# A lag on the inputs of ScalarE's casts in a list schedule: attention followed by a gated two-layer network, on one core

## The chip, the cores and the metric

The kernel runs on one core of one Trainium2 chip. The core has five engines that work side by side, each through its own queue in the order in which the program wrote it: TensorE (PE in the profile, with PEld for its weight loads), VectorE (DVE), ScalarE (ACT), GpSimd (POOL) and SyncE (SP), which here only issues the transfers (DMA) between DRAM and on-chip memory. The metric is the time of one execution on the device in microseconds (us); less is better.

## The reference

```python
# q, k, v: (8 batches, 8 heads, 576 rows, 64); tau = 0.02
scores = q @ k.T / sqrt(64)
scores = where(scores >= max(scores) - tau, scores, -1e9)      # only the top band survives
attn   = exp(scores - max(scores)); attn = attn / (sum(attn) + 1e-9)
x      = (attn @ v)  ->  (4608 tokens, 512)                     # heads side by side
gate   = sigmoid(x @ w_gate); val = x @ w_val                   # w_gate, w_val: 512 x 1536
out    = (gate * val) @ w_out                                   # w_out: 1536 x 512
```

The kernel writes `out` transposed, 512 x 4608. Everything is float32; a product that must keep float32's precision is made of three products of halves: a value is split into a rounded high part and the rest, and high x high, high x low and low x high are added up.

## The kernel before

**The work.** Attention goes through 32 visits: 8 batches `b` times 4 pairs of heads `hp`. A visit has 9 tiles of 128 queries. For each tile TensorE makes the scores (`s`, line 661), VectorE their negative maximum (`st`, 668), ScalarE the exponentials (`p`, 682), VectorE the mask and the row sums (685), TensorE transposes `p` in four pieces (`tp`, 767) and ScalarE copies the transposed block out of PSUM (`pt`, 718); every second tile TensorE multiplies with `v` (`av`, 803), and ScalarE copies that to `xf` (718 again). Scores, transposes and `av` share a few PSUM banks: the next one can only start once ScalarE or VectorE has emptied a bank. In the text a visit is named by its two numbers, so (5, 0) is batch 5, pair 0.

Beside attention, TensorE works through the gated network (`m`, line 863, and `o`, line 906) for batches 0, 1 and 2, in units of 12 matmuls of 512 columns with one weight tile each (`wi`, `wo`, 512 KB, streamed from DRAM through nine slots `w`). When attention ends, the other batches follow in three rounds of two batches at a time (lines 1105 and 1170), by Strassen's scheme in Winograd's form, with seven products in place of eight.

**The sums.** That scheme needs sums and differences of weight blocks. They are made on the way: while batches 1 and 2 go through `m`, and batches 0 and 1 through `o`, two weight tiles that have been streamed anyway are also read by POOL, which makes two new tiles of them (`s0_...`, `s1_...`, also in `w` slots) in six additions (line 957). Then ScalarE rounds each new tile to its high part (the cast of line 968), POOL subtracts that from the tile (969), and SP stores the result in DRAM (lines 977 and 989). There are 18 such sums, so 36 casts. The operations of a sum have the key 1000, lower in priority than attention's and higher than the network's.

**x read back.** For batch 2 the attention result goes to DRAM (`xa`, line 1271), comes back into a `t2` buffer (1301), and is split into high and low part by `split_x`: a cast on ScalarE (813) and a subtraction on POOL (815). There are 4 such casts. For batches 0 and 1 the same function reads `xf` without a detour (8 casts).

**What sets the order.** The program is not written in the order in which it runs. Each operation is recorded by `op(engine, cost, key, ...)` with the buffers that it reads and writes. `Plan.run` then plays a list schedule: it keeps a clock, counts an engine as busy for the recorded cost, and on each engine starts the ready operation with the lowest key whose buffers have room. An operation becomes ready when the last of its inputs is done, plus a lag: `LAG` for the engine (0.3 for ScalarE) plus the operation's own `lag`, which no operation of the kernel before sets. The order of starts is the order in which the program is then written. On the chip each engine goes through its queue in that order, whatever the real times are: an instruction that has to wait holds everything behind it on its engine.

```python
for s in x.succ:
    lag = 0.0 if s.eng == x.eng else LAG[s.eng]
    s.ready = max(s.ready, now + lag + s.lag)
```

Of the kernel before, what the change touches and what calls it, by code (L numbers as in the profile page):

```python
# [20 lines left out]
def f32(ap):  # L21
    return ap.bitcast(F32)
# [21 lines left out]
class Plan:  # L44
# [10 lines left out]
    def buf(self, tag, shape, dtype, name, cls=None):  # L55
        return Buf(self, tag, shape, dtype, name, cls)
# [9 lines left out]
    def op(self, eng, cost, key, emit, reads=(), writes=(), also=(), leave=0, behind=None, after=(), lag=0.0):  # L66


        o = Op()
        o.eng, o.cost, o.emit, o.key, o.leave, o.lag = eng, cost, emit, key, leave, lag  # L70
        o.succ, o.seq, o.ready = [], len(self.ops), 0.0
        deps, bufs = set(after), []
        for group, write in ((reads, False), (writes, True)):
            for x in group:
                b, part = x if isinstance(x, tuple) else (x, None)
                for q, p, w in b.accesses:
                    if (write or w) and (p is None or part is None or p == part):
                        deps.add(q)
                if b not in bufs:
                    bufs.append(b)  # L80
        for group, write in ((reads, False), (writes, True)):
            for x in group:
                b, part = x if isinstance(x, tuple) else (x, None)
                b.accesses.append((o, part, write))
        for b in bufs:
            b.users += 1
        deps.discard(o)
        o.n_deps, o.next = len(deps), None
        if behind is not None:
            o.n_deps += 1  # L90
            behind.next = o
        for q in deps:
            q.succ.append(o)
        o.bufs, o.also = bufs, [b for b in also]
        self.ops.append(o)
        return o
# [191 lines left out]
TWOS = ((3, 4), (5, 6), (7, 8))  # L288

SUMS_IN, SUMS_OUT, SUM_KEY = {1: (0,), 2: (1,)}, {0: (0,), 1: (1,)}, 1000  # L290

AWAY = 2
AHEAD_TWO = 8
# [5 lines left out]
def act(n):  # L299
    return 0.19 + 0.0008 * n  # L300
# [6 lines left out]
def pool(n):  # L307
    return 0.2 + 0.0022 * n
# [7 lines left out]
def kernel(  # L316
# [25 lines left out]
    nc = tc.nc  # L342
# [10 lines left out]
    SM = NJ * P  # L353
# [81 lines left out]
    op, buf = plan.op, plan.buf  # L435
# [373 lines left out]
               reads=[pt, pl] + ([c.pt, c.pl] if last else []) + [vis.vs], writes=[av], also=[vis.xf])  # L809
            last_att[0] = copy(AV(vis.first), W, key, lambda: vis.xf.ap[:, c0 : c0 + W], av, (vis.xf, self.name))  # L810

    def split_x(x, c0, c1, xf, key):
        op("ACT", act(c1 - c0), key, lambda: nc.scalar.copy(x.ap[:, 0, c0:c1], xf.ap[:, : c1 - c0]),
           reads=[xf], writes=[(x, (0, c0))])
        op("POOL", pool(c1 - c0), key, lambda: nc.gpsimd.tensor_tensor(
            out=x.ap[:, 1, c0:c1], in0=xf.ap[:, : c1 - c0], in1=f32(x.ap[:, 0, c0:c1]), op=ALU.subtract
        ), reads=[xf, (x, (0, c0))], writes=[(x, (1, c0))])
# [110 lines left out]
    def streamed(blk, tag=""):  # L928
        return lambda f, i: stream(
            wi_d[f, i], lambda: wi_d[f, i].t.rearrange("p z c f -> p (z c f)"), f"wi{blk}_{f}_{i}{tag}"  # L930
        )
# [19 lines left out]
    def sums(name, x_u, x_v, full, half, put):  # L951

        u, v = (buf("w", [P, 2 * DM], F32R, f"s{j}_{name}") for j in range(2))
        key = SUM_KEY

        def add(cost, out, x, y, sign, reads, writes):
            op("POOL", cost, key, lambda: nc.gpsimd.tensor_tensor(  # L957
                out=f32(out()), in0=f32(x()), in1=f32(y()), op=ALU.add if sign > 0 else ALU.subtract
            ), reads=reads, writes=writes)

        for t, x in ((u, x_u), (v, x_v)):
            add(1.3, lambda t=t: full(t, 0), lambda x=x: full(x, 0), lambda x=x: full(x, 1), 1, [x], [t])
        add(1.0, lambda: half(u, 1, 0), lambda: half(v, 0, 0), lambda: half(v, 0, 1), 1, [v], [u])
        add(1.0, lambda: half(u, 1, 1), lambda: half(u, 1, 0), lambda: half(u, 0, 0), -1, [], [u])
        add(1.0, lambda: half(v, 1, 0), lambda: half(u, 0, 0), lambda: half(v, 0, 0), -1, [u], [v])
        add(1.0, lambda: half(v, 1, 1), lambda: half(u, 0, 1), lambda: half(u, 1, 1), -1, [u], [v])
        for k, t in enumerate((u, v)):
            op("ACT", act(512), key, lambda t=t: nc.scalar.copy(full(t, 0), f32(full(t, 1))), writes=[t])
            op("POOL", 1.3, key, lambda t=t: nc.gpsimd.tensor_tensor(
                out=full(t, 1), in0=f32(full(t, 1)), in1=f32(full(t, 0)), op=ALU.subtract  # L970
            ), writes=[t])
            put(k, t, key)

    def in_sums(f, i, u, v):
        def put(k, t, key):
            d = si_d[f, i, k]
            op("SP", 1.7, key, lambda: nc.sync.dma_start(
                out=d.t.rearrange("p z c f -> p (z c f)"), in_=f32(t.ap)
            ), reads=[t], writes=[d])

        view = lambda t: t.ap.rearrange("p (z c f) -> p z c f", z=2, c=ND)
        sums(f"{f}_{i}", u, v, lambda t, z: view(t)[:, z], lambda t, z, h: view(t)[:, z, 2 * h : 2 * h + 2], put)

    def out_sums(g, e, u, v):
        view = lambda t: t.ap.rearrange("p (f z c) -> p f z c", f=ND, z=2)

        def put(k, t, key):
            d = so_d[g, k]
            op("SP", 1.7, key, lambda: nc.sync.dma_start(
                out=d.t[:, :, e].rearrange("p s f z c -> p s (f z c)"),  # L990
                in_=f32(t.ap).rearrange("p (s f z c) -> p s (f z c)", s=2, f=2, z=2),
            ), reads=[t], writes=[(d, e)])

        sums(f"o{g}_{e}", u, v, lambda t, z: view(t)[:, :, z], lambda t, z, h: view(t)[:, 2 * h : 2 * h + 2, z], put)
# [233 lines left out]
    t = 0  # L1228
# [8 lines left out]
    xs, gs = {}, {}  # L1237
# [7 lines left out]
    def attention(vis):  # L1245
        vis.prepare(LEAD)
        t, c, groups = vis.first, None, []
        for h, tiles in vis.groups:
            g = Group(vis, h, tiles)
            groups.append((g, t))  # L1250
            for i in range(g.n):
                tile_steps(vis, g, i, t + i)
            t += g.n
            g.normalise(t - 1)
            for i in range(g.n):
                g.transpose(i, t - 1 + 0.1 * i)
            if h is None:
                c = g
            g.leftover_keys(t - 1 + 0.2)
            if h == 1:  # L1260
                g.output(c, t - 1 + 0.3)
        if vis.late:
            late_normalise(vis, t)
        b, hp = vis.b, vis.hp
        if b in two_of:
            i, j = two_of[b]
            op("SP", 0.9, t, lambda i=i, j=j: nc.sync.dma_start(
                out=xp_d[i][hp].t[:, :, j], in_=vis.xf.ap[:, :SM].rearrange("p (z s) -> p z s", z=2)
            ), reads=[vis.xf], writes=[(xp_d[i][hp], j)])
        elif b >= AWAY:  # L1270
            op("SP", 0.9, t, lambda: nc.sync.dma_start(out=xa_d[b, hp].t, in_=vis.xf.ap[:, :SM]),
               reads=[vis.xf], writes=[xa_d[b, hp]])
        else:
            xs[b, hp] = buf("x", [P, 2, SM], F32R, f"x{b}_{hp}")
            split_x(xs[b, hp], 0, SM, vis.xf, t)
        i, j = two_of[B]
        SQ = SL // 2
        op("SP", 0.3, t, lambda: nc.sync.dma_start(
            out=xp_d[i][hp].t[:, :, j, b * SQ : (b + 1) * SQ],
            in_=vis.xf.ap[:, SM:].rearrange("p (z s) -> p z s", z=2),  # L1280
        ), reads=[vis.xf], writes=[(xp_d[i][hp], (j, b))])

    def block(b):
        return [xs[b, hp] for hp in range(NPAIR)]

    def new_g(b):
        gs[b] = [buf("g", [P, 2, SM], F32R, f"g{b}_{f}") for f in range(NF)]
        return gs[b]
# [4 lines left out]
    for vis in todo:  # L1293
        attention(vis)
        b = vis.b
        if vis.hp == NPAIR - 1 and b not in two_of:
            if b >= AWAY:
                for hp in range(NPAIR):
                    xf = buf("t2", [P, SM], F32, f"xa{b}_{hp}")
                    xs[b, hp] = buf("x", [P, 2, SM], F32R, f"x{b}_{hp}")  # L1300
                    op("SP", 1.0, 0.5, lambda xf=xf, b=b, hp=hp: nc.sync.dma_start(out=xf.ap, in_=xa_d[b, hp].t),
                       reads=[xa_d[b, hp]], writes=[xf], also=[xs[b, hp]])
                    split_x(xs[b, hp], 0, SM, xf, 0.5)
            in_units(b, block(b), new_g(b), 0, SM, 0, own if b == 0 else streamed(b))
            out_units(b, gs[b])
    for i in range(len(TWOS)):
# [80 lines left out]
```

## Time and profile before

| What | Value |
|---|---|
| time, median of 3 runs | 1363.42 us (1363.32 to 1367.26) |
| profiled execution | span 1362.5 us from its first to its last instruction; the profile gives no other time of it |
| busy: PE, PEld, DVE, ACT, POOL | 1323.1, 1089.2, 942.9, 726.4, 452.9 us |
| mean granted TensorE clock | 0.992 |
| DMA | 322.37 MB, mean 237 GB/s |
| attention and network together | up to about 828 us |
| rounds of two batches | from 844 us on |

A row of a timeline has the start and the length in us, the engine, the source line, the operation, what it writes and reads, the shape and the count; brackets give how long the engine stood idle just before, and what ended that. A row of a window table has the stretch, its length, then for each engine the busy time and the number of instructions, and at the end the granted TensorE clock (1.00 is full speed), the share of time in which the 16 DMA engines were busy, and their rate in GB/s. A row of waits has who waited for whom, the total in us, how many times, and the longest. Names in the profile have their numbers left out (`s` for a sum's tile and also for scores: the line tells them apart).

### The profile page before, as it was taken

The page shows a single profiled execution, that of the slowest core. Times are in us where ns is not written, and L with a number is a line of the kernel's source. Part 1 is how long each engine was busy: PE and PEld are TensorE (multiplying, and loading weights), DVE is VectorE, ACT ScalarE, POOL GpSimd, SP SyncE. Part 2 cuts the span into 40 slices and gives each one's busy share as a digit, 9 for nine tenths or more (in the row PEclk, how much of TensorE's full clock was granted, in tenths as well). Part 3 has the DMA queues.
Part 4 walks back from the last instruction along what each step waited for, and adds up shares of the span by engine and source line. Part 5 has one row for each costly group of instructions (what it writes and reads, how often), then busy time and mean ns, then how long its engine had stood idle before and what let it go on. Part 6 is the DMA issues. An engine that isn't in the chain of part 4 may idle for free.

```text
span 1362.5 us, 23334 instructions
## 1 busy us (share of the span) xinstructions
PE 1323.1 (97%) x8290; PEld 1089.2 (80%) x8290; DVE 942.9 (69%) x1848; ACT 726.4 (53%) x1339; POOL 452.9 (33%) x419
## 2 busy tenths in 40 slices
PE   8879999999999998999999999999999999999998
PEld 5557888888877887888878887888888888888887
DVE  7888878677766775677667772746965569655594
ACT  7887777666666765666666552222532225322242
POOL 3575756714444532634544421111000110001100
PEclk9998999999999999999989999999999999999999
DMA  7799999899788787898788777765685656756563
GB/s 267 242 282 312 332 255 284 278 257 263 227 244 248 230 243 224 239 274 260 219 250 261 221 210 244 246 205 188 216 292 195 196 189 219 238 193 190 189 217 123
DMA packets 151612, 322.37 MB, mean 237 GB/s; under 512 B 30152, under 2 KB 57800, under 8 KB 151496
## 3 DMA queue, kind: packets, MB, share of 16 engines
q1 hardware_dynamic: 151352, 320.88, 76.6%
q8 instruction: 66, 1.08, 0.3%
q14 instruction: 50, 0.41, 0.1%
q10 hardware_dynamic: 144, 0.00, 0.0%
HBM read 212.93 MB, written 54.67 MB: 196 GB/s over the span
## 4 chain that ended last, share of the span: by engine, by line
PE 80%; DMA 9%; SPq 4%; ACT 2%; DVE 2%; issue 2%; POOL 2%; POOLq 0%; ACTq 0%; DVEq 0%
PE m L863 11%; PE qb L1105 11%; PE av L803 8%; PE qa L1105 7%; PE qc L1105 7%; PE s L661 7%; PE o L906 6%; PE tp L767 6%; PE rb L1170 5%; PE rc L1170 4%; PE ra L1170 4%; DMA rd<-turned 1%; PE s_l L661 1%; DMA xp<-xf 1%; DMA kd<-k 1%
## 5 line engine op out<-in xcount | busy, mean ns | idle before, releaser
L668 DVE TENSOR_REDUCE st<-s 128x1 f32<-128x576 f32 x256 | 192.2, 752 | 98.7 <-PE s L661 92.1
L685 DVE SCALAR_TENSOR_TENSOR p<-s,st,p 128x576 f32<-128x576 f32 x256 | 207.2, 812 | 45.5 <-ACT p L682 40.5
L682 ACT ACTIVATE p<-s,st 128x576 f32<-128x576 f32 x256 | 191.1, 749 | 32.8 <-DVE st L668 32.2
L718 ACT COPY pt<-tp 128x512 f32<-128x512 f32 x256 | 149.1, 586 | 96.3 <-PE tp L767 95.0
L661 PE MATMUL s<-kd,qd 128*128 128x288 f32 x928 | 169.4, 306 | 5.1 <-DVE p L685 4.3
L863 PE MATMUL m<-x,wi 128*128 128x512 f32 x576 | 165.5, 409 | 1.4 <-ACT pt L718 1.4
L767 PE MATMUL tp<-ident,p 128*128 128x128 f32 x1024 | 157.4, 278 | 7.0 <-ACT xf L718 3.8
L1018 POOL TENSOR_TENSOR gA<-gA 128x512 f32<-128x512 f32 x18 | 24.1, 1341 | 406.8 <-DVE gA L1084 406.8
L661 PEld LDWEIGHTS s<-kd,qd 128*128 128x128 f32 x928 | 141.6, 190 | 20.0 <-DVE p L685 5.7
L767 PEld LDWEIGHTS tp<-ident,p 128*128 128x128 f32 x1024 | 122.1, 142 | 31.3 <-issue 6.4
L803 PE MATMUL av<-pt,vs 128*64 128x256 f32 x1024 | 126.2, 389 | 1.5 <-ACT pt L718 1.3
L906 PE MATMUL o<-g,wo 128*128 128x512 f32 x432 | 119.7, 405 | 0.0
L863 PEld LDWEIGHTS m<-x,wi 128*128 128x128 f32 x576 | 99.4, 190 | 14.5 <-ACT pt L718 1.8
L1105 PE MATMUL qa<-xs_p,wa 128*128 128x512 f32 x432 | 109.5, 389 | 0.0
L803 PEld LDWEIGHTS av<-pt,vs 128*64 128x64 f32 x1024 | 68.6, 138 | 48.5 <-issue 10.2
L1042 DVE TENSOR_TENSOR qu<-qb,qp 128x512 f32<-128x512 f32 x72 | 49.6, 691 | 80.6 <-PE qb L1105 69.3
L1105 PEld LDWEIGHTS qa<-xs_p,wa 128*128 128x128 f32 x432 | 81.1, 188 | 16.8
L906 PEld LDWEIGHTS o<-g,wo 128*128 128x128 f32 x432 | 75.9, 190 | 11.0 <-issue 0.2
L863 PE MATMUL m<-x,ws 128*128 128x512 f32 x288 | 80.4, 412 | 0.6 <-ACT pt L718 0.5
L713 POOL TENSOR_TENSOR xf<-xf,rb 128x576 f32<-128x576 f32 x31 | 44.9, 1448 | 92.0 <-DMA rb<-rd 62.3
L957 POOL TENSOR_TENSOR s<-wi 128x512 f32<-128x512 f32 x24 | 33.0, 1376 | 106.8 <-DMA wi<-wid 101.9
L1010 ACT CAST gs_p<-gA 128x512 fp32r<-128x512 f32 x54 | 32.8, 620 | 61.2 <-DVE gA L1084 23.0
(145 smaller groups left out, 2516.9 us busy)
## 6 DMA issues: line engine op xcount, KB each, us to landing
kd<-k SPq DMA_DIRECT2D x116, 320.0 KB
wi<-wid SPq DMA_DIRECT2D x48, 512.0 KB
wo<-wod SPq DMA_DIRECT2D x36, 512.0 KB
wa<-wid SPq DMA_DIRECT2D x36, 512.0 KB
ws<-sid SPq DMA_DIRECT2D x36, 512.0 KB
wt<-sid SPq DMA_DIRECT2D x36, 512.0 KB
wo_p<-sod SPq DMA_DIRECT2D x36, 512.0 KB
qd<-q SPq DMA_DIRECT2D x116, 128.0 KB
```

The lines of the kernel that those rows point to most:

```text
L661: nc.tensor.matmul(s.ap[:, c, :HALF], st(), mv(slice(kc + c * HALF, kc + (c + 1) * HALF)), start=m == 0, stop=m == len(steps) - 1,)
L668: op("DVE", 0.76, key, lambda: nc.vector.tensor_reduce(out=st.ap[:, 0:1], in_=sv(), axis=AX.XY, op=ALU.max, negate=True), reads=[s], write ...
L682: op("ACT", 0.74, key, lambda: nc.scalar.activation(p(), sv(), AF.Exp, bias=st.ap[:, 0:1], scale=1.0), reads=[s, (st, 0)], writes=[(g.p, i)])
L685: op("DVE", 0.9, key, lambda: nc.vector.scalar_tensor_tensor(out=p(), in0=sv(), scalar=st.ap[:, 1:2], in1=p(), op0=ALU.is_ge, op1=ALU.mult ...
L718: return op("ACT", act(n), key, lambda: nc.scalar.copy(dst(), src.ap), reads=[src], writes=[part])
L767: nc.tensor.matmul(tp.ap[:, c, :], self.p.ap[:, o + c * P : o + (c + 1) * P], ident, is_transpose=True, start=c == 0, stop=c == NJ - 1, sk ...
L803: nc.tensor.matmul(av.ap[h * D : (h + 1) * D, a:z], vis.vs.ap[:, j, h], m(h), start=i == 0, stop=i == len(ms) - 1, skip_group_check=True,)
L863: nc.tensor.matmul(m.ap, wv[:, a, c * P : (c + 1) * P], xs[c].ap[:, z, c0:c1], start=e == 0, stop=e == 11,)
L906: nc.tensor.matmul(acc.ap, wv[:, f, a], g[fg * ND + f].ap[:, z], start=(fg, f, a, z) == (0, 0, 0, 0), stop=(fg, f, a, z) == (NFG - 1, ND - ...
L1042: f = lambda: nc.vector.tensor_tensor(out=out.ap, in0=ps_[bank].ap, in1=x.ap, op=ALU.add)
L1105: nc.tensor.matmul(acc.ap, wv[:, y, (2 * h + c) * P : (2 * h + c + 1) * P], xt[prod][c].get()[:, z], start=e == 0 and prod in FIRST, stop= ...
L1170: nc.tensor.matmul(acc.ap, w.ap[:, e, c, y], gt[prod][2 * g + c].get()[:, z], start=m == 0 and g == 0 and prod in FIRST, stop=m == 5 and g ...
```

## The change

Two constants are added, both 6.0. The casts of the sums get the lag `LATE_SUMS`, and the casts of x read back get `LATE_LOAD`: the schedule counts them as ready 6 us later than before. `split_x` passes a lag on; its other call leaves it at zero. Nothing is computed otherwise, and no instruction is added or taken away.

```diff
+LATE_SUMS, LATE_LOAD = 6.0, 6.0
...
-    def split_x(x, c0, c1, xf, key):
+    def split_x(x, c0, c1, xf, key, lag=0.0):
         op("ACT", act(c1 - c0), key, lambda: nc.scalar.copy(x.ap[:, 0, c0:c1], xf.ap[:, : c1 - c0]),
-           reads=[xf], writes=[(x, (0, c0))])
+           reads=[xf], writes=[(x, (0, c0))], lag=lag)
...
-            op("ACT", act(512), key, lambda t=t: nc.scalar.copy(full(t, 0), f32(full(t, 1))), writes=[t])
+            op("ACT", act(512), key, lambda t=t: nc.scalar.copy(full(t, 0), f32(full(t, 1))), writes=[t], lag=LATE_SUMS)
...
-                    split_x(xs[b, hp], 0, SM, xf, 0.5)
+                    split_x(xs[b, hp], 0, SM, xf, 0.5, LATE_LOAD)
```

The change moves far more than the 40 casts. Since buffers come free at other times, the list schedule deals out all engines anew from the first cast on: the orders of all five engines are the same up to about 242 us of the trace, differ from there to the end of attention, and agree again a few matmuls into the first round of two batches. Every line behind the new constants has a number higher by two. In the rows below the first number of a name is left out, and the last one is a serial number that differs between the two programs.

The first place is ScalarE's queue at the cast of x read back for pair 2 (`x_2`), while attention passes from visit (4, 3) to (5, 0). Before:

```order
L885 CAST g_11_6692<-th_11_0_6618 128x512
L682 ACTIVATE p_0_00_6707<-s_0_000_6666,st_0_000_6697 128x576
L718 COPY xf_3_6716<-av_3_10_6676 128x256
L813 CAST x_2_6722<-xa_2_6671 128x512
L718 COPY pt_3_02_6571<-tp_3_120_6702 128x4x128
L718 COPY pt_3_02_6571<-tp_3_121_6724 128x4x128
L576 CAST k_1_6746<-kn_1_6545 128x640
L718 COPY pl_3_02_6600<-lk_3_12_6744 128x128
L813 CAST x_3_6763<-xa_3_6690 128x512
```

After:

```order
L720 COPY xf_3_6721<-av_3_10_6692 128x256
L720 COPY pt_3_02_6583<-tp_3_121_6715 128x4x128
L720 COPY pl_3_02_6613<-lk_3_12_6730 128x128
L578 CAST k_1_6748<-kn_1_6508 128x640
L580 ACTIVATE q_1_6755<-qn_1_6519,scale_t 128x640
L684 ACTIVATE p_0_00_6709<-s_0_001_6723,st_0_001_6740 128x576
L720 COPY pt_0_00_6788<-tp_0_000_6743 128x4x128
L684 ACTIVATE p_0_l_6791<-s_0_l_6733,st_0_l_6751 128x576
L720 COPY xf_3_6721<-av_3_12_6757 128x320
L815 CAST x_2_6808<-xa_2_6652 128x512
L720 COPY pt_0_00_6788<-tp_0_001_6812 128x4x128
```

The cast stood behind the copy of the first half of visit (4, 3)'s output (`av_3_10`); now it stands behind that of the second half (`av_3_12`), eight rows further on, with two transposed blocks, two exponentials and the split of the next visit ahead of it.

The second place is ScalarE's queue at the two casts of the sum `4_1` (of weight tiles 4 and 6, batch 2), during visit (6, 2). Before:

```order
L877 ACTIVATE th_4_0_8774<-m_4_0_0_8642 128x512
L718 COPY pt_2_02_8792<-tp_2_020_8781 128x4x128
L968 CAST s_4_1_8516<-s_4_1_8516 128x512
L682 ACTIVATE p_2_10_8810<-s_2_100_8766,st_2_100_8790 128x576
L718 COPY pt_2_02_8792<-tp_2_021_8801 128x4x128
L718 COPY pl_2_02_8822<-lk_2_02_8808 128x128
L682 ACTIVATE p_2_10_8810<-s_2_101_8794,st_2_101_8806 128x576
L968 CAST s_4_1_8683<-s_4_1_8683 128x512
```

After:

```order
L720 COPY pt_2_02_8774<-tp_2_020_8763 128x4x128
L684 ACTIVATE p_2_10_8792<-s_2_100_8749,st_2_100_8772 128x576
L720 COPY pt_2_02_8774<-tp_2_021_8785 128x4x128
L720 COPY pl_2_02_8805<-lk_2_02_8794 128x128
L684 ACTIVATE p_2_10_8792<-s_2_101_8778,st_2_101_8790 128x576
L879 ACTIVATE th_4_0_8818<-m_4_0_0_8742 128x512
L720 COPY pt_2_00_8665<-tp_2_100_8821 128x4x128
L970 CAST s_4_1_8552<-s_4_1_8552 128x512
L684 ACTIVATE p_2_12_8847<-s_2_120_8813,st_2_120_8829 128x576
```

The first cast moved from ahead of the exponentials `p_2_10` to behind them and behind the copy of the next transposed block (`tp_2_100`).

The third place is ScalarE's queue at the first casts of the first round of two batches (`xs_p`, read from `xb`), which the change does not touch itself, near the passage from visit (7, 2) to (7, 3). Before:

```order
L718 COPY xf_2_10204<-av_2_10_10180 128x256
L718 COPY pt_2_02_10086<-tp_2_120_10199 128x4x128
L718 COPY pt_2_02_10086<-tp_2_121_10213 128x4x128
L682 ACTIVATE p_3_00_10232<-s_3_000_10206,st_3_000_10218 128x576
L1010 CAST xs_p_0_10240<-xb_0_0_10157 128x512
L682 ACTIVATE p_3_00_10232<-s_3_001_10222,st_3_001_10234 128x576
L1010 CAST xs_p_1_10269<-xb_1_0_10081 128x512
```

After:

```order
L887 CAST g_9_10132<-th_9_0_10060 128x512
L1012 CAST xs_p_0_10154<-xb_0_0_10099 128x512
L720 COPY xf_2_10162<-av_2_10_10134 128x256
L720 COPY pt_2_02_10038<-tp_2_120_10156 128x4x128
L1012 CAST xs_p_1_10179<-xb_1_0_10012 128x512
L720 COPY pt_2_02_10038<-tp_2_121_10172 128x4x128
L684 ACTIVATE p_3_00_10197<-s_3_000_10164,st_3_000_10177 128x576
```

The first cast now stands ahead of the copy of `av_2_10`, which it followed by four rows before.

## The prediction

> **What bounds the kernel now.** I read the busy times first, then two stretches of a window table, since the change moves nothing ahead of 240 us and nearly nothing behind 846 us.
>
> ```profile
> PE 1323.1 (97%) x8290; PEld 1089.2 (80%) x8290; DVE 942.9 (69%) x1848; ACT 726.4 (53%) x1339; POOL 452.9 (33%) x419
> 240.00:846.00 606.00, 590.00 (x4449) 493.71 (x4448) 414.95 (x944) 377.05 (x709) 254.91 (x220) 0.99 0.83 245
> ```
>
> TensorE bounds the kernel. In the stretch that the change reorders it stands idle for 606.0 - 590.0 = 16.0 us, and its work there is the same before and after. So the first question is whose wait these 16 us are. TensorE's own timeline has six idle gaps of more than 0.7 us in the stretch:
>
> ```profile
> 354.58 0.73 PE L863 MATMUL m<-x,wi 128*128 128x512 f32 x2 [1.35 <-ACT pt L718]
> 390.07 0.66 PE L767 MATMUL tp<-ident,p 128*128 128x128 f32 x4 [2.60 <-ACT xf L718]
> 423.94 0.65 PE L767 MATMUL tp_l<-ident,p_l 128*128 128x128 f32 x4 [1.95 <-ACT pt L718]
> 518.90 0.48 PE L780 MATMUL lk<-ident,p 128*128 128x128 f32 x1 [4.54 <-ACT pt L718]
> 552.89 0.66 PE L767 MATMUL tp_l<-ident,p_l 128*128 128x128 f32 x4 [0.76 <-ACT pt L718]
> 683.47 0.85 PE L661 MATMUL s<-kd,qd 128*128 128x288 f32 x2 [3.08 <-DVE p L685]
> ```
>
> They add up to 1.35 + 2.60 + 1.95 + 4.54 + 0.76 + 3.08 = 14.28 us, nine tenths of the idle time. Each is ended by a ScalarE copy, or by VectorE's mask, which needs ScalarE's exponentials. ScalarE's timeline just ahead of each gap shows what held ScalarE:
>
> ```profile
> 352.79 0.62 ACT L968 CAST s<-s 128x512 fp32r<-128x512 f32 x1 [1.82 <-POOL s L957]
> 387.98 1.14 ACT L968 CAST s<-s 128x512 fp32r<-128x512 f32 x2 [3.46 <-POOL s L957]
> 422.27 1.14 ACT L968 CAST s<-s 128x512 fp32r<-128x512 f32 x2 [2.51 <-POOL s L957]
> 517.75 0.62 ACT L813 CAST x<-xa 128x512 fp32r<-128x512 f32 x1 [5.77 <-DMA xa<-xa]
> 551.21 1.14 ACT L968 CAST s_o<-s_o 128x512 fp32r<-128x512 f32 x2 [1.33 <-POOL s_o L957]
> 681.29 0.62 ACT L968 CAST s<-s 128x512 fp32r<-128x512 f32 x1 [3.63 <-POOL s L957]
> ```
>
> The reader is to see that all six are the casts that get the lag: ScalarE, busy 53%, stands in front of a cast whose input POOL or a transfer has not finished, and the copies and exponentials behind it, for which TensorE waits, could have run. All waits of this kind, and the chain that ended last, which names TensorE for four fifths and so says little of its gaps:
>
> ```profile
> ACT s L968 <- POOL s L957: 18.6, 10, 3.6
> ACT s_o L968 <- POOL s_o L957: 1.3, 1, 1.3
> ACT x L813 <- DMA xa<-xa: 6.8, 3, 5.8
> PE 80%; DMA 9%; SPq 4%; ACT 2%; DVE 2%; issue 2%; POOL 2%; POOLq 0%; ACTq 0%; DVEq 0%
> ```
>
> So 26.7 us of ScalarE's waits are worth 14.28 us to TensorE, and two of the gaps cost clock afterwards. This is read from narrow windows behind the gaps:
>
> ```profile
> 391.00:395.00 4.00, 4.00 (x36) 3.03 (x36) 3.14 (x8) 3.75 (x7) 1.85 (x2) 1.00 0.88 348
> 519.00:523.00 4.00, 3.99 (x15) 2.86 (x17) 1.59 (x3) 4.00 (x8) 3.67 (x3) 0.62 0.17 38
> 684.00:690.00 6.00, 6.00 (x25) 5.17 (x24) 3.33 (x8) 2.33 (x5) 2.50 (x2) 0.56 1.05 258
> ```
>
> After the gap of 2.60 us the granted clock stays at 1.00; after those of 4.54 and 3.08 us it is 0.62 for 4 us and 0.56 for 6 us. That is TensorE time lost besides the gap: 4 x 0.38 + 6 x 0.44 = 4.16 us.
>
> **The change part by part.** It adds and removes no instruction; the casts, their POOL subtractions and the stores behind these stay the same number and size. What changes is where they stand in the queues.
>
> *The casts move back.* The new place is measured by the time at which the row now ahead of the cast ended in the trace. For the first and second place shown above, and for the cast at 387.98, which now follows the second output copy of its visit:
>
> ```profile
> 395.94 0.42 ACT L718 COPY xf<-av 128x320 f32<-128x320 f32 x1 [1.20 <-PE av L803]
> 525.60 0.43 ACT L718 COPY xf<-av 128x320 f32<-128x320 f32 x1 [2.48 <-PE av L803]
> 686.54 0.59 ACT L718 COPY pt<-tp 128x512 f32<-128x512 f32 x1 [1.68 <-PE tp L767]
> ```
>
> The inputs were there at 387.98, 517.75 and 681.29 us, the starts of the waiting casts; the new places end at 396.36, 526.03 and 687.13, that is 8.4, 8.3 and 5.8 us later. But those places come nearer once the gap itself is gone: taking off 2.60, then 4.54 + 1.5 of clock, then 3.08 + about 1.4 of clock, a margin of 5.8, 2.3 and 1.4 us is left. All are above zero, so I count the six gaps as gone: -14.28 us, and their clock with them: -4.16 us. Bounds: none of it (0) if inputs come later by the margins, all of it (-18.44). I take all, since the least margin is still positive, and put the doubt into the chances.
>
> On the clock the Trainium skill ("TensorE: Matmul & The Clock Gate", Part 1) states that the array falls to half rate only after an idle window of about 3.4 us. The trace agrees for the gap of 4.54 us and differs for the one of 3.08 us, after which the clock fell as well. By the page's rule the 6 us at 0.56 would have another cause and stay, 2.64 us less gain, about 1353 us in place of the sum below; the measurement decides here.
>
> *POOL's subtraction (line 969) waits for the later cast.* It was in front of ScalarE's cast already at times:
>
> ```profile
> POOL s L969 <- ACT s L968: 10.0, 11, 2.1
> ACT xs_p L1010 <- DMA xb<-xp: 3.5, 2, 3.2
> ```
>
> Behind it in POOL's queue stand the split of the next visit's `k`, the normalising of `xf` and the network's low parts. POOL is busy 254.9 of 606 us here, and the schedule puts the subtraction behind the cast, so I count 0; bounds 0 and +10.0, the sum of today's waits going on to TensorE in full. Without POOL's spare time the split of `k`, and the scores after it, would be late.
>
> *The stores and the `w` slots.* A sum's two tiles keep two of nine slots some 6 us longer and so hold back the next weight loads; this is hidden while TensorE does not wait for `wi` or `wo`. It does not now (gap 1.4 us in all on `m`, ended by ScalarE):
>
> ```profile
> L863 PE MATMUL m<-x,wi 128*128 128x512 f32 x576 | 165.5, 409 | 1.4 <-ACT pt L718 1.4
> ```
>
> I count 0 (bounds 0 and what the third rival below says).
>
> *Scores of visit (2, 2) move ahead.* At the first place where TensorE's order differs, its first scores from `kd` stand where the ones from `k` stood, at 261.18 us; `kd` is sent from 254.80 on, and a `kd` transfer took 7.14 us.
>
> ```profile
> 254.80 1.28 SPq L597 DMA_DIRECT2D kd<-k  x1
> 258.73 7.14 DMA kd<-k
> 261.18 1.05 PE L661 MATMUL s_l<-k,q 128*128 128x288 f32 x6
> ```
>
> 254.80 + 7.14 = 261.94 to 256.08 + 7.14 = 263.22 us, so 0.8 to 2.0 us late; two stores of sums (512 KB each) now come after it instead of before, which brings it forward. I take +0.5, between 0 and +2.0.
>
> *The first `xs_p` cast moves ahead of an output copy* (third place). It waited for its transfer before, at small cost to TensorE:
>
> ```profile
> 791.75 8.68 DMA xb<-xp
> 794.51 0.37 ACT L718 COPY xf<-av 128x256 f32<-128x256 f32 x1 [3.06 <-PE av L803]
> 800.46 0.62 ACT L1010 CAST xs_p<-xb 128x512 fp32r<-128x512 f32 x1 [3.17 <-DMA xb<-xp]
> 802.73 0.63 PE L767 MATMUL tp<-ident,p 128*128 128x128 f32 x4 [0.41 <-DVE p L685]
> ```
>
> ScalarE stood 3.17 us, TensorE 0.41 us. Now the cast comes about 3 us sooner (794.5 against 797.3) and holds a copy that frees a PSUM bank, as at 387.98, where 3.46 us on ScalarE became 2.60 us on TensorE. One store of a sum and one weight tile less are ahead of its transfer, 1 MB or about 4 us at the 245 GB/s of the stretch, so its wait should stay near 3 us. I take +2.0, between 0.4 less than nothing (today's gap goes) and +4.5 (a wait of 6 us at the ratio 2.60 / 3.46).
>
> *All other rows dealt anew.* No row shows what else will meet. Bounds: -1.7 (16.0 - 14.28, all other idle time goes) and +13.35, what TensorE stood idle in the stretch where transfers lead:
>
> ```profile
> 30.00:100.00 70.00, 56.65 (x489) 40.34 (x484) 59.28 (x123) 55.97 (x108) 46.07 (x59) 0.98 0.87 258
> ```
>
> I take +3.0, nearer the low end, since outside the six gaps the present deal of the same work lost only 1.7 us in 606.
>
> Sum: -14.28 - 4.16 + 0.5 + 2.0 + 3.0 = -12.9 us. 1362.5 - 12.9 = 1349.6 us of span; the median of the runs is 0.9 us above the profiled span, so 1350.5 us.
>
> **The rivals.** *First, the waits only move.* The lag is a guess by a schedule whose transfers are faster than the chip's; the casts may wait at new places, or other copies behind `xs_p` and `k` casts may. For it: the margin of 1.4 us at 681 is thin. Against it: every one of the six casts moves back by 5 us or more. If two thirds of the lost time come back, the time is 1363.4 - 18.4 / 3 = 1357.3; if all of it does and the 3 us of the rows dealt anew come on top, 1366.4; the middle is 1362.
>
> *Second, all of the gain and nothing new:* 1363.4 - 18.4 = 1345.0 us. For it: the reordered rows hold the same work and one engine with 97% busy. Against it: the third place above.
>
> *Third, slower: weights late.* With slots held longer, 26 of the 192 weight loads stand nearer to their first matmul in the new orders, those of the last `o` units among them. If each made TensorE wait, the 18.4 us would be eaten up at 0.7 us apiece; 1 us gives 1363.4 - 18.4 + 26 = 1371, and 1.5 us 1384. It decides from 0.87 us a load on (22.5 us, the gain and 0.3%). For it: the DMA engines are busy 83% of the stretch. Against it: no row has TensorE waiting for a weight tile there now.
>
> **How the numbers follow.** 0.3%, 4.1 us, is about what a measurement of this kernel can tell from no change. Forecast (1346 to 1357): 0.63. First rival (1357.3 to 1366.4): 0.17, of which 0.03 is faster than 1359.3 and 0.14 the same. Second (1344 to 1346): 0.08. Third (1367.5 to 1384): 0.12, taken whole as slower. So faster 0.63 + 0.08 + 0.03 = 0.74, same 0.14, slower 0.12. The range leaves out the third rival and a little at both ends of the others: 1344.5 to 1362.5, and the likeliest case alone is 1346 to 1357.
>
> **What would show it.** Right: ScalarE's waits in front of lines 970 (casts of sums) and 815 (x read back) fall from 19.9 and 6.8 us to under 3 together; TensorE's idle time in 240 to 846 us falls from 16.0 to about 7; the granted clock has no window under 0.8 in the stretch; and the first matmul of the rounds, at 844.16 us (827.99 + 16.17) now, comes some 13 us sooner:
>
> ```profile
> 827.99 16.17 PE L906 MATMUL o<-g,wo 128*128 128x512 f32 x70
> ```
>
> Wrong: a gap at the first `xs_p` cast above 4.5 us, any TensorE wait on `wi` or `wo`, a clock dip in a new place, or long POOL waits at line 971 with a `k` split behind them.

## The result, and the profile after

The changed kernel is slower: median 1374.49 us (13 runs, 1368.07 to 1375.8) against 1363.91 us for the kernel before (13 runs on the same chip, 1355.0 to 1368.37). The ratio is 1.0064, 95% interval 1.0044 to 1.0085. The forecast was 1350.5 us. The profiled execution is the median one: span 1372.7 us, 10.2 us longer than that of before. Busy times of the page, and the window table for the start, the reordered stretch, and the two windows in which the clock had dipped before:

```profile
PE 1325.4 (97%) x8290; PEld 1090.9 (79%) x8290; DVE 940.3 (69%) x1848; ACT 727.6 (53%) x1339; POOL 449.2 (33%) x419
0.00:240.00 240.00, 219.66 (x1562) 170.04 (x1563) 193.41 (x402) 184.53 (x346) 141.67 (x159) 0.96 0.89 278
240.00:846.00 606.00, 582.91 (x4425) 488.32 (x4424) 414.98 (x954) 379.30 (x712) 255.27 (x223) 0.99 0.83 241
519.00:523.00 4.00, 1.78 (x35) 1.54 (x30) 2.74 (x4) 3.80 (x7) 1.68 (x2) 0.95 0.97 339
684.00:690.00 6.00, 6.00 (x47) 4.75 (x45) 4.75 (x13) 4.30 (x9) 3.73 (x4) 1.00 0.99 251
```

The work is the same, but TensorE stands idle for 606.0 - 582.91 = 23.1 us of the stretch instead of 16.0. The clock dips in the two old windows are gone. The waits table of the changed kernel names what came:

```profile
POOL s L971 <- ACT s L970: 18.8, 8, 8.2
PE s L663 <- DVE p L687: 11.8, 13, 2.6
ACT xs_p L1012 <- DMA xb<-xp: 11.8, 2, 11.6
ACT k L578 <- DMA kd<-k: 11.1, 5, 2.8
PE tp L769 <- ACT xf L720: 10.2, 3, 8.9
PE s L663 <- DMA kd<-k: 3.0, 2, 1.8
```

There is no row any more with ScalarE waiting in front of line 970 or 815: the change does what it says, and all six old gaps are gone. ScalarE now stands in front of other casts, which wait for transfers: the split of `k` (line 578) and the first cast of the rounds (line 1012). The largest place, in the timelines of ScalarE, TensorE and SP and the last step of the chain of waits:

```profile
784.54 0.62 ACT L887 CAST g<-th 128x512 fp32r<-128x512 f32 x1
790.41 0.38 SPq L1202 DMA_DIRECT2D xb<-xp  x1
790.41 6.30 DMA xb<-xp
796.73 0.62 ACT L1012 CAST xs_p<-xb 128x512 fp32r<-128x512 f32 x1 [11.57 <-DMA xb<-xp]
797.25 0.37 ACT L720 COPY xf<-av 128x256 f32<-128x256 f32 x1
787.98 0.77 PE L663 MATMUL s<-kd,qd 128*128 128x288 f32 x4
797.67 0.69 PE L769 MATMUL tp<-ident,p 128*128 128x128 f32 x2 [8.92 <-ACT xf L720]
```

ScalarE reached the cast at 785.16 us, SP issued its transfer at 790.41, and it landed 6.30 us later. So 5.25 of the 11.57 us passed before the transfer was sent at all: from 781.50 us on SP issued one transfer after another with less than 0.1 us between them. Whether SP's issuing or the bytes in its queue were the limit there was not tested. Behind the cast stood the output copy, and TensorE stood 8.92 us for that. The clock fell with it (window table, five columns of busy time, then the clock):

```profile
792.00:796.00 4.00, 0.00 (x0) 0.00 (x0) 0.00 (x0) 0.00 (x0) 0.00 (x0) 0.53 1.04 374
796.00:800.00 4.00, 2.33 (x10) 2.33 (x11) 1.77 (x4) 3.07 (x6) 0.00 (x0) 0.50 0.96 374
800.00:804.00 4.00, 4.00 (x20) 2.48 (x21) 3.13 (x7) 1.29 (x3) 1.28 (x1) 0.69 0.28 104
```

The busy time at less than full clock costs 2.33 x 0.50 + 4.00 x 0.31 = 2.4 us more. A smaller place of the other kind, again ScalarE and then TensorE:

```profile
518.76 0.73 ACT L578 CAST k<-kn 128x640 fp32r<-128x640 f32 x1 [2.59 <-DMA kd<-k]
520.13 0.72 ACT L684 ACTIVATE p<-s,st 128x576 f32<-128x576 f32 x1
522.68 1.30 PE L663 MATMUL s<-kd,qd 128*128 128x288 f32 x4 [2.21 <-DVE p L687]
512.93 1.40 SPq L599 DMA_DIRECT2D kd<-k  x1
```

The split of `k` waits 2.59 us, and the row names `kd<-k`: a transfer of the visit before, which by the program reads the same buffer that the split writes (`k2` has one slot). It was sent at 512.93 us, the split's own load of `k` already at 505.00, so the load is probably not what was late. The exponentials stand behind the split, the mask needs these, and the next scores wait for the PSUM bank that the mask empties.

### The profile page after: what moved, and what is told of

The parts are those of the page before. It is cut to its first block, busy times and chain, and to the rows that moved or that the text cites. A ratio compares the mean times of both kernels' runs of the same rounds, so it can differ in the third digit from the quotient of the medians.

```text
span 1372.7 us, 23351 instructions
## 1 busy us (share of the span) xinstructions
PE 1325.4 (97%) x8290; PEld 1090.9 (79%) x8290; DVE 940.3 (69%) x1848; ACT 727.6 (53%) x1339; POOL 449.2 (33%) x419
## 4 chain that ended last, share of the span: by engine, by line
PE 80%; DMA 7%; SPq 5%; DVE 3%; ACT 2%; issue 2%; POOL 0%; DVEq 0%; POOLq 0%; ACTq 0%
PE m L865 12%; PE qb L1107 11%; PE av L805 8%; PE s L663 7%; PE qa L1107 7%; PE qc L1107 7%; PE tp L769 6%; PE o L908 6%; PE rb L1172 5%; PE rc L1172 4%; PE ra L1172 4%; DMA wi<-wid 2%; DMA kd<-k 1%; DVE p L687 1%; SPq L599 1%
## 5 line engine op out<-in xcount | busy, mean ns | idle before, releaser
L769 PE MATMUL tp<-ident,p 128*128 128x128 f32 x1024 | 158.3, 279 | 12.1 <-ACT xf L720 10.2
L769 PEld LDWEIGHTS tp<-ident,p 128*128 128x128 f32 x1024 | 123.5, 142 | 37.2 <-ACT xf L720 10.0
L805 PEld LDWEIGHTS av<-pt,vs 128*64 128x64 f32 x1024 | 68.8, 138 | 50.5 <-issue 12.3
```

The costliest lines, as they stand in the source:

```text
L769: nc.tensor.matmul(tp.ap[:, c, :], self.p.ap[:, o + c * P : o + (c + 1) * P], ident, is_transpose=True, start=c == 0, stop=c == NJ - 1, sk ...
L805: nc.tensor.matmul(av.ap[h * D : (h + 1) * D, a:z], vis.vs.ap[:, j, h], m(h), start=i == 0, stop=i == len(ms) - 1, skip_group_check=True,)
```

## The experiments

Theory A: each wait that the lag removes passes to the next cast that depends on a transfer, so those casts are the loss. Theory B: the lag on x read back alone carries it. Theory C: transfers run late by an amount that any order waits out somewhere. Theory D: any new deal of the order has such waits, and the kernel before is one of the better deals. Eighteen kernels were run, four or two at a time, each group beside the kernel before (medians 1364.5, 1364.9, 1363.9, 1361.9 and 1364.1 us).

### Each half of the change

```diff
-LATE_SUMS, LATE_LOAD = 6.0, 6.0
+LATE_SUMS, LATE_LOAD = 6.0, 0.0     # sums only; 0.0, 6.0 for x read back only
```

> Half of the change: the lag of 6.0 on the casts of the weights' sums alone, none on the casts of x read back. Theory A (the waits that the lag removes pass to the next ScalarE casts that are fed by a load: the split of k and the first cast of the rounds): the scheduler gives the first cast of the rounds 5.5 us of its own time behind its load, near the 5.1 of the changed kernel and below the 8.1 of the kernel before, so a TensorE gap of 5 to 9 us stands there again and the time is 1366 to 1374. Theory B (the loss hangs on the lag of x read back, which takes slots of x and moves the reads): without it 1353 to 1360. Theory C (the transfers alone set the pace, whatever the order): 1370 to 1376, with the same gap of about 9 us before the rounds.

Measured: 1373.5 us, ratio 1.0076 (1.0051 to 1.0101), TensorE idle 17.2 us in the stretch in the profiled execution (whose span, 1369.0, is one of the shorter), and 2.4 us more just behind 846 us, at casts of the rounds.

> The other half: the lag on the casts of x read back alone, none on the sums. Theory A: the gap of 4.54 us with its clock dip goes (about 6 us), the five gaps before casts of sums (9.74 us together in the kernel before) stay, and the first cast of the rounds has 6.1 us behind its load in the scheduler's time, so 2 to 7 us of wait there: 1360 to 1366. Theory B: it carries the loss: 1370 to 1376. Theory C: 1362 to 1368, no part matters by itself.

Measured: 1367.9 us, ratio 1.0030 (1.0011 to 1.0049), idle 19.6 us. B falls, since the sums' half alone is as slow as the whole. A's sizes are not met either, nor is C's gap of about 9 us: with the lag on the sums alone TensorE's gap at the first cast is only 3.5 us, and the largest waits are TensorE's own for `kd`:

```profile
PE s L663 <- DMA kd<-k: 9.9, 2, 6.1
```

### The first cast of the rounds moved by hand

The program gets a function that takes a recorded operation, and what uses it, out of the finished order and puts it back some ScalarE rows later.

```diff
         self.time = now
+        self.behind(order, <the first two casts to xs_p>, 16)
         for o in order:
             o.emit()
```

> The changed kernel's order with one piece moved by hand: the first two ScalarE casts of the rounds (with the VectorE subtractions that use them, and one of GpSimd) stand 15 ScalarE rows later; every other row of all engines stays. Theory A: the 9.08 us gap at 788 us and the clock of 0.50 to 0.69 behind it go, 9.1 and about 4 us, and nothing needs these casts before the rounds begin near 844: 1374.5 - 13 = 1361.5, range 1359 to 1364. Theory C: the load still lands at its time and the next user of a load waits in its place: 1370 to 1375.

Measured: 1369.5 us, ratio 1.0030 (1.0009 to 1.0051): 5.0 us better than the changed kernel, not 13. A window row and three timeline rows of this run (its line numbers are 18 higher):

```profile
792.00:796.00 4.00, 4.00 (x48) 3.78 (x45) 1.79 (x4) 2.24 (x4) 0.00 (x0) 1.00 0.97 369
802.18 1.43 POOL L733 TENSOR_TENSOR xf<-xf,rb 128x576 f32<-128x576 f32 x1 [17.01 <-DMA rb<-rd]
802.39 3.44 DVE L1034 TENSOR_TENSOR xs_p<-xb,xs_p 128x512 fp32r<-128x512 f32 x2 [0.80 <-ACT xs_p L1030]
806.62 1.33 PE L681 MATMUL s<-kd,qd 128*128 128x288 f32 x4 [2.73 <-DVE p L705]
```

The gap and its dip are gone (792 to 796: TensorE busy throughout, clock 1.00), so the cast was their cause. But 2.73 us came back where the two moved subtractions now hold VectorE at 1.72 us apiece, and ScalarE still waits some 21 us in front of splits of `k`. Neither theory had this time: A said 1359 to 1364, C 1370 to 1375.

### The splits moved too

```diff
+        self.behind(order, <first cast to xs_p>, 17); self.behind(order, <second>, 6)
+        for n in (10, 17, 18, 22, 26):
+            self.behind(order, <casts that split k and q of visit n>, 4)
```

> The changed kernel's order with single pieces moved by hand: the first two ScalarE casts of the rounds stand 17 and 6 ScalarE rows later, and at five places the two casts that split k and q stand 4 ScalarE rows later, behind the exponentials and copies that waited behind them. Nothing else moves but what uses them. Theory A (each wait passes to the next cast fed by a load): the gaps before the scores, 13.7 us in nine places with the first casts moved alone, fall to under 5 us, the one at the first casts stays gone, and the time falls from 1369.5 to 1357 to 1362. Theory C (the transfers set the pace): k is split later, kd is read back later, and TensorE waits for kd in their place: 1367 to 1372.

Measured: 1376.5 us, ratio 1.0082 (1.0052 to 1.0111), idle 27.8 us: worse than with the first casts alone by 7 us, and above the ranges of both theories. At a split that had not been moved (line numbers 22 higher):

```profile
648.65 0.72 ACT L599 CAST k<-kn 128x640 fp32r<-128x640 f32 x1 [7.57 <-DMA kd<-k]
651.90 1.30 PE L685 MATMUL s<-kd,qd 128*128 128x288 f32 x4 [6.53 <-DVE p L709]
```

The move itself is a reason. Counted from the last row of ScalarE whose order is common (242.86 us here, 246.73 in the changed kernel), ScalarE came to this place 0.9 us later than in the changed kernel, but this load of `k` was sent 5.4 us later (at 627.63 against 626.09 us), since `kn` has one buffer and GpSimd had first to finish the subtraction behind a split that had been moved:

```profile
SPq L589 <- POOL k L604: 3.7, 1, 3.7
```

SP stood 3.7 us for that, and what follows in its queue came later too. So this run does not show that A is wrong: a split moved back also holds back the next load.

### More lags, and earlier loads

```diff
-            op("ACT", 0.73, key, ... reads=[kn], writes=[(k2, 0)])
+            op("ACT", 0.73, key, ... reads=[kn], writes=[(k2, 0)], lag=6.0)   # also the cast of q and the first casts of the rounds
```

> The changed kernel, with the lag of 6.0 also on the casts that split k and q and on the first casts of the rounds, so that all of ScalarE's casts fed by a load have it. The order is dealt anew from the third pair on. Theory A: the gaps of 9.08 us and the four of 2.4, 2.0, 1.3 and 1.35 us before casts of k go with their clock dips (13 + 7 + 3): 1350 to 1356, unless kd, read back later by then, makes TensorE wait for the scores (the scheduler itself plans 1355 for this kernel and 1344 for the changed one): then 1357 to 1366. Theory C: 1370 to 1376.

Measured: 1379.1 us, ratio 1.0109 (1.0083 to 1.0136), idle 22.2 us.

```diff
-            op("SP", 1.2, key - 4, ...    # loads of k and q
+            op("SP", 1.2, key - 12, ...   # and lag 6.0 on the first casts of the rounds
```

> The changed kernel with the loads of k and q ranked earlier in the queue of transfers (12 instead of 4 steps ahead), and the lag of 6.0 on the first casts of the rounds: the scheduler then gives a split of k at least 18 us behind its load's issue (13.4 to 23.3 in the changed kernel) and the first cast of the rounds 15.2 us instead of 5.1. Theory A: gaps before the scores behind a split of k fall under 4 us and the one before the rounds goes: 1354 to 1361. Theory C: what is loaded earlier delays another load (weights, kd, x): 1366 to 1376. Theory D: 1368 to 1379, whatever the distances.

Measured: 1378.2 us, ratio 1.0107 (1.0068 to 1.0145), idle 20.5 us. The casts wait little now (9 us in all, counting waits of 0.3 us and more), but TensorE itself stands for `kd`:

```profile
PE s L663 <- DMA kd<-k: 14.4, 5, 5.8
```

### Deals without a purpose, and the lag on top of them

```diff
-LAG = {"PE": 0.8, "DVE": 0.2, "ACT": 0.3, "POOL": 0.3, "SP": 0.08}
+LAG = {"PE": 0.8, "DVE": 0.2, "ACT": 0.3, "POOL": 0.31, "SP": 0.08}   # second: ACT 0.31; third: ACT 0.29
```

> The kernel before without the change, with one constant of the scheduler moved by a trifle (its time from a result to GpSimd, 0.30 to 0.31), which deals the order anew and has no purpose. Theory A: the casts keep the distances to their loads that they had, 9.3 us for the first cast of the rounds against 8.1, so the time stays within the scatter of a like order: 1360 to 1369. Theory D (any new deal of the order moves the waits to other places, and the kernel before is one of the better deals): like the four deals so far, 1368 to 1379, mean 1373.7.

> The same with the scheduler's time from a result to ScalarE, 0.30 to 0.31: a second deal without a purpose. The scheduler itself plans 1352 for it, 1348 for the kernel before and for the first neutral deal. Theory A: 1360 to 1371. Theory D: 1368 to 1379.

> A third neutral deal of the kernel before, ScalarE's time 0.30 to 0.29, no lag. Theory D: 1368 to 1379 like the other two (1373.7 and 1372.6). If deals scatter around the kernel before, and the two were chance: 1355 to 1367.

Measured: 1373.7, 1372.6 and 1377.3 us, ratios 1.0060 (1.0038 to 1.0081), 1.0052 (1.0031 to 1.0073) and 1.0097 (1.0069 to 1.0124). A change of 0.01 us in one constant costs as much as the change under study.

> The change on top of the first neutral deal (GpSimd's time 0.31, both lags 6.0). The deal without the lag measured 1373.7, with 29.5 us of ScalarE's waits before the casts in question. Theory E (the lag gains what the prediction counted, and the kernel before only hid it by being one of the better deals): those waits fall under 4 us and the time to 1356 to 1364. Theory D (a deal has 16 to 28 us of TensorE idle between 240 and 846 us whichever casts have a lag): the waits fall as well, but the time is 1367 to 1380.

> The change on top of the second neutral deal (ScalarE's time 0.31), which measured 1372.6 without it, with 34.5 us of waits before these casts. Theory E: 1355 to 1363. Theory D: 1367 to 1380. The first cast of the rounds has 5.5 us behind its load in the scheduler's time, near the changed kernel's 5.1, so a gap there is likely by either.

> The change on top of the third neutral deal. The scheduler itself plans 1344.1 against 1349.7 without the lag, the same promise as for the change (1343.7 against 1348.3). Theory E: 8 to 15 us faster than the third neutral deal. Theory D: within 6 us of it, either side.

Measured: 1378.3, 1371.5 and 1370.9 us. With the lag less without it, the four pairs give +10.6 (the change itself), +4.6, -1.0 and -6.4 us, mean +1.9. Two of these pairs were measured in different groups; by the ratios to the kernel before in each group they are +8.7, +7.0, +1.9 and -6.0 us, mean +2.9. So E falls, and the lag as such has no effect that four pairs show. The lag did its work in each, as the waits tables of the first neutral deal without and with it show:

```profile
ACT s L968 <- POOL s L957: 16.3, 7, 5.5
ACT x L813 <- DMA xa<-xa: 7.8, 4, 4.1
ACT s_o L968 <- POOL s_o L957: 5.4, 3, 3.9
```

```profile
ACT s_o L970 <- POOL s_o L959: 0.5, 1, 0.5
ACT s L970 <- POOL s L959: 0.3, 1, 0.3
PE s L663 <- DMA kd<-k: 15.8, 4, 6.2
ACT xs_p L1012 <- DMA xb<-xp: 7.6, 2, 6.7
```

Added up from the traces between 240 and 846 us (waits of 0.3 us and more, in us):

| Kernel | time | casts of sums, x back | splits of k, q | casts to xs_p | PE on transfers | sum | PE idle |
|---|---|---|---|---|---|---|---|
| before | 1363.9 | 26.8 | 4.0 | 3.9 | 0.0 | 34.6 | 16.0 |
| changed | 1374.5 | 0.0 | 21.6 | 17.8 | 3.0 | 42.5 | 23.1 |
| neutral 1 | 1373.7 | 29.5 | 7.0 | 5.1 | 0.0 | 41.7 | 21.2 |
| neutral 1, lag | 1378.3 | 0.5 | 12.3 | 8.6 | 15.8 | 37.2 | 23.4 |
| neutral 2 | 1372.6 | 33.9 | 6.9 | 0.0 | 1.2 | 42.0 | 20.6 |
| neutral 2, lag | 1371.5 | 3.0 | 18.9 | 9.8 | 3.1 | 34.8 | 20.4 |
| neutral 3 | 1377.3 | 21.1 | 9.5 | 4.1 | 0.0 | 34.7 | 21.1 |
| neutral 3, lag | 1370.9 | 1.8 | 22.8 | 4.9 | 7.1 | 36.7 | 22.5 |

In these eight kernels the sum stays at 35 to 42 us; the lag changes who waits. The sum does not rank them, though: the kernel before and the third neutral deal have nearly the same sum, with 16.0 and 21.1 us idle. (The third neutral deal and the second with the lag have about 2.5 us more of idle time just behind 846 us.)

### Fewer bytes in the same orders

Each sum's store writes only a sixteenth of it (the diff shows one of the two kinds of stores), and the rounds load plain weights in place of the sums, as many bytes as before. So these kernels leave out most of the sums, and what they compute is not the reference. No instruction is added, taken away or moved.

```diff
-                out=d.t.rearrange("p z c f -> p (z c f)"), in_=f32(t.ap)
+                out=d.t.rearrange("p z c f -> p (z c f)")[:, :64], in_=f32(t.ap)[:, :64]
```

> The kernel before with a sixteenth of each of the 36 stores of the weights' sums to DRAM (512 KB each, 17.7 MB less of the about 148 MB moved between 240 and 846 us); the rounds load the plain weights in their place, as many bytes as before. The order of every engine is that of the kernel before. Theory C: the waits on transfers go, the waits of the casts for GpSimd stay: TensorE idle from 16 to 10 to 14 us, 1358 to 1363. Theory D: 1362 to 1367.

> The changed kernel with the same stores cut to a sixteenth, in its own order. Theory C: its waits are all for transfers (21.6 us before splits of k, 17.8 before first casts of the rounds, 3.0 of TensorE itself), so most of them go: TensorE idle from 23 to 6 to 12 us and the time from 1374.5 to 1350 to 1361, below the light kernel before. Theory D: 1369 to 1376.

> The first neutral deal with the same stores cut. Theory C: it loses only the part of its waits that is on transfers, 12 of 42 us: from 1373.7 to 1366 to 1372. Theory D: 1370 to 1376.

> The first neutral deal with the lag and the same stores cut. Theory C: from 1378.3 to 1354 to 1365, since nearly all of its 37 us of waits are on transfers; the lag then pays by what the prediction counted. Theory D: 1373 to 1380.

Measured: 1348.2, 1351.1, 1356.3 and 1347.6 us: 15.7, 23.4, 17.4 and 30.7 us less than the medians of the same four orders with whole stores (which are from other groups; against the kernel before of its own group, the first is 13.7 us less). Three of the four lie below C's ranges, all below D's. The window rows of the light kernels, in this order:

```profile
240.00:846.00 606.00, 601.50 (x4516) 503.85 (x4515) 426.57 (x959) 385.13 (x723) 262.42 (x223) 1.00 0.78 221
240.00:846.00 606.00, 597.53 (x4457) 501.52 (x4456) 430.97 (x961) 384.65 (x721) 254.07 (x217) 1.00 0.79 223
240.00:846.00 606.00, 597.60 (x4493) 498.79 (x4493) 423.37 (x952) 383.91 (x721) 269.36 (x229) 1.00 0.78 223
240.00:846.00 606.00, 604.98 (x4541) 505.73 (x4540) 425.10 (x961) 387.75 (x727) 267.99 (x230) 1.00 0.80 225
```

TensorE's idle time falls from 16.0, 23.1, 21.2 and 23.4 us to 4.5, 8.5, 8.4 and 1.0. D alone cannot do that with no row of an engine moved, so most of the idle time depends on the bytes of the transfers (a store also keeps its `w` slot, so late loads and late slots are not told apart). C did not foresee that the casts of sums gain as well: their waits in the kernel before fall from 20.0 to 5.9 us, so part of what looked like POOL being late was POOL's own late inputs. With light transfers the lag pays on the first neutral deal (8.7 us; ratios to the kernel before 0.9888, 0.9862 to 0.9915, against 0.9954, 0.9931 to 0.9976) and makes no difference that shows on the deal of before (0.9900, 0.9867 to 0.9932, against 0.9894, 0.9864 to 0.9924).

### An order dealt for slower transfers

```diff
-                        dma = max(now + 1.5, dma) + got.cost
+                        dma = max(now + 1.5, dma) + got.cost * (1.15 if now > 240 else 1.0)
```

> The kernel before, with the scheduler counting every transfer 15 per cent longer from its 240th us on: no instruction less, another order. It then gives a split of k 20 to 30 us behind its load's issue (13.6 to 23.5 before). Theory C in the form that the transfers' lateness is fixed and must be waited out somewhere, whatever the order: 1366 to 1380, like the other deals. If the order can hide it once the scheduler knows of it: 1348 to 1362.

> The changed kernel with the same longer transfers in the scheduler, splits of k 20 to 32 us behind their loads. Theory C in the strict form: 1366 to 1380. If the order can hide the lateness: 1345 to 1358, below the run without the lag.

Measured: 1370.2 us, ratio 1.0043 (1.0027 to 1.0059), and with the lag 1387.0, ratio 1.0167 (1.0137 to 1.0196). The first time lies in C's range of 1366 to 1380, the second above it. Two window rows of the run without the lag, then the stretch from 690 us of the network's `m` matmuls alone (line 863; columns: busy, clock, DMA share, rate), in the kernel before and in this one:

```profile
240.00:690.00 450.00, 448.57 (x3330) 380.00 (x3327) 292.57 (x669) 286.32 (x546) 224.16 (x201) 1.00 0.94 261
690.00:846.00 156.00, 139.95 (x1127) 115.52 (x1126) 110.15 (x272) 91.69 (x164) 24.06 (x17) 1.00 0.71 195
```

```profile
690.00:846.00 156.00, 44.36 (x162) 1.00 0.79 240
```

```profile
690.00:846.00 156.00, 0.00 (x0) 1.00 0.71 195
```

For 450 us this order hides the transfers: TensorE idle 1.4 us at a DMA share of 0.94. It does so by putting the network's matmuls sooner into attention, and none of the `m` ones are left from 690 us on, where TensorE then waits 16.1 us, 13.7 of it for masks (VectorE) between scores. A second wait comes just behind the stretch, at a first cast of the rounds:

```profile
PE qb L1105 <- ACT xs_p L1010: 6.9, 1, 6.9
```

With the lag it is 4.3 us idle up to 690, 21.4 from there to 846, and 5.8 us at the same cast. So C's reason fails: the lateness of the transfers is not a fixed amount in any order. A milder factor, or one that ends sooner, was not tried; none of the kernels with all the bytes beats the one before.

## Why the prediction was wrong

**What bounds the kernel, and the six gaps: right as far as it went.** TensorE bounds it, and the -14.28 us were real: none of the six gaps and none of their waits is left.

**The clock: right for the old dips, missed for new ones.** The 4.16 us went, and 4.8 us came: 2.4 us at 796 to 804, and behind the gaps before scores at 522.68 and 574.29 us 1.78 x 0.18 + 4 x 0.25 + 1.71 x 0.28 + 4 x 0.15 = 2.4 us (rows of TensorE's window table and timeline):

```profile
520.00:524.00 4.00, 1.78 (x22) 0.82 0.80 283
524.00:528.00 4.00, 4.00 (x21) 0.75 0.21 72
572.00:576.00 4.00, 1.71 (x6) 0.72 0.91 315
576.00:580.00 4.00, 4.00 (x24) 0.85 0.68 185
574.29 1.30 PE L663 MATMUL s<-kd,qd 128*128 128x288 f32 x4 [2.58 <-DVE p L687]
```

**The first `xs_p` cast: mis-sized.** Forecast +2.0, at most +4.5; measured 8.92 us and 2.4 us of clock. The transfer did come 3.7 us sooner (796.71 against 800.43), as reckoned. But ScalarE was at the cast 12.1 us sooner (785.16 against 800.46 - 3.17 = 797.29), not 3. The forecast timed the place by the old row at 794.51 us, which itself says that ScalarE had stood idle 3.06 us before it; and attention came to this place about 7 us sooner, because the new order has 8.3 us fewer of the network's matmuls ahead of it (240.9 us of `m` and `o` between the last common row of ScalarE and this place, 249.2 before).

**All other rows dealt anew: the step that failed.** I took +3.0, since "outside the six gaps the present deal of the same work lost only 1.7 us". Idle outside the old gaps and the first cast is now 23.1 - 8.9 = 14.2 us, so the term was 14.2 - 1.7 = +12.5, near the upper bound of +13.35 (with the 1.79 us at visit (2, 2) below). Nearly all of it is ten gaps of 0.4 us or more, 13.4 us together: two of scores that wait for `kd`, eight of scores that wait for a mask, each of them just after ScalarE had stood 0.8 to 3.0 us in front of a split of `k`. The 1.7 us was a property of one good deal. Three deals without a purpose have 20.6 to 21.2 us idle and a mean of 1374.5 us; the four with the full lag, 1373.8. In sum -14.28 + 8.92 + 12.5 = +7.1 us idle, the clock +0.6. Up to the copy below the orders are the same (kernel before, then changed):

```profile
242.87 0.37 ACT L718 COPY xf<-av 128x256 f32<-128x256 f32 x1 [2.48 <-issue]
246.73 0.37 ACT L720 COPY xf<-av 128x256 f32<-128x256 f32 x1 [2.48 <-POOL s_o L959]
```

So 3.9 of the 10.2 us lie ahead of all that the change moves. That part is chance of the execution: in three other runs whose order up to here is that of the changed kernel, the same copy starts at 240.62, 242.86 and 237.03 us. From this copy to the first matmul of the rounds it is 601.1 us before and 607.8 after, 6.7 more. The medians differ by 10.6 us, so one profile of each does not account for all of the difference; the other executions were not profiled.

**POOL, the slots, the scores of visit (2, 2).** POOL's waits behind the later casts rose from 10.0 to 18.8 + 6.4 us without a gap of TensorE that ends on them, so 0 fits. The first scores of visit (2, 2) from `kd` waited for their load within the bounds of 0 and +2.0, near the upper one and not at the +0.5 taken:

```profile
267.07 0.77 PE L663 MATMUL s<-kd,qd 128*128 128x288 f32 x4 [1.79 <-DMA kd<-k]
```

**The rivals.** The third has the right sign and a time that fits, by a mechanism that is not there: no gap waits for `wi` or `wo`. The first named what happened ("other copies behind `xs_p` and `k` casts may" wait), but capped it at 1366.4, by what the old waits had cost. Nothing bounds new waits by old ones. Its remark that the schedule's transfers are faster than the chip's fits what the runs show, and deserved a larger share: cutting 17.7 MB of transfers takes 15.7 to 30.7 us from four orders in which no engine's row moved. But a schedule that counts the transfers longer was not faster either.

**The signs.** Right: the casts' waits under 3 us. Wrong: idle 23.1 instead of 7, a window of 0.50, and the first matmul of the rounds at 854.55 us, over 10 us later instead of 13 sooner:

```profile
854.55 1.52 PE L1107 MATMUL qa<-xs_p,wa 128*128 128x512 f32 x6
```

## What to carry to other kernels

Where a scheduler deals the whole order anew, first measure what a deal without a purpose does: here 0.01 us in a constant cost 8 to 13 us, as much as the change, and one good profile says nothing of the next deal. Follow a wait to what is late (here transfers, at a DMA share of 0.83) before moving the instruction that stands in front of it; in an in-order queue the next one with a late input takes its place. Time a moved instruction by what stands ahead of it in the new order, not by the old trace's clock.

## What the runs showed of the hardware

At a DMA share of 0.83 over 606 us, 12% fewer bytes (share 0.78 to 0.80) cut TensorE's idle time by 11 to 22 us; but the order dealt for slower transfers ran 450 us at a share of 0.94 with 1.4 us idle, so the mean share alone does not say whether transfers come late. The clock fell to 0.82 and 0.75 behind a gap of 2.21 us, to 0.72 and 0.85 behind one of 2.58, and not at all behind one of 2.60 in the kernel before, so the gap's length alone does not decide. The Trainium skill ("TensorE: Matmul & The Clock Gate", Part 1) has the array fall to half rate only after an idle window of about 3.4 us; these rows differ from that, and the measurement decides. And a VectorE subtraction of 128x512 that takes 0.69 us as a rule took 1.72 us twice in a row while GpSimd was working beside it at 802 us; that GpSimd was the reason was not tested.
